# Feature map from two elementwise steps, and block-diagonal k^T v by one masked product, in a fused linear attention and expert kernel

## The chip, the cores and the metric

The kernel runs on one core of a Trainium2 chip, as one program and one launch. The metric is the device time in microseconds (us) from the first to the last instruction of that core; the time of a kernel is the median of its runs. A core has five engines with queues of their own: TensorE (PE in the profile) for matmuls, VectorE (DVE), ScalarE (ACT), GpSimd (POOL) and SyncE (SP), which here only starts transfers. Each engine works through its own list of instructions in a fixed order.

## The reference: what is computed

Linear attention over 8 batches x 8 heads x 576 tokens x 64 channels, and then a layer of 8 experts, in which every token goes through all experts and the results are weighted by a matrix P. P comes from a Sinkhorn normalisation: eight rounds of dividing rows and columns by their sums.

```python
def phi(x):
    return np.where(x > 0, x, np.exp(x) - 1.0) + 1.0
q_p, k_p = (phi(q), phi(k))
kv = np.einsum('bhsd,bhse->bhde', k_p, v)
z = np.sum(k_p, axis=2)
num = np.einsum('bhsd,bhde->bhse', q_p, kv)
den = np.einsum('bhsd,bhd->bhs', q_p, z)[..., None] + 1e-06
return (num / den).astype(np.float32)
...
logits = x @ w_gate          # x: the attention's output, 4608 tokens x 512
P = np.exp(logits - logits.max())
for _ in range(8):
    P /= P.sum(1, keepdims=True) + 1e-09
    P /= P.sum(0, keepdims=True) + 1e-09
    P *= N / E
for e in range(E):           # 8 experts
    h = np.maximum(x @ w1[e], 0.0)
    out += P[:, e:e + 1] * (h @ w2[e])
```

The feature map phi(x) is x + 1 where x is positive and exp(x) elsewhere. It can be written without a comparison, in two ways: max(x + 1, min(exp(x), 1)) and min(exp(x), max(x + 1, 1)). For x > 0 both give x + 1, since exp(x) is the larger; for x <= 0 both give exp(x).

## The kernel before

The kernel has two parts. In the **front** the attention runs in 16 groups of four heads (two groups for each batch), and expert 0 runs between them as plain matmuls, so that PE has work while the other engines prepare the next group. After the front, experts 1 to 7 run in a form with fewer multiplications (Strassen's: seven block products in place of eight, with sums of blocks built by DVE); these are the lines L640 and L843 of the profile. A small planner in the kernel places each piece of work on an engine and in an order, from a table of priorities (`ranks`) at its end; where a piece names two engines, the planner or the table chooses.

One group of the attention, with cuts. The load, the feature map of k and of q, and v:

```python
# p_in, p_t, p_vv ...: pools of two buffers each; e: three
(nc.gpsimd if n in (2, 3) else nc.sync).dma_start(out=gr["tile"]..., in_=AP(...))   # k, q, v of the group
...
def f_e(_, ge=ge, nm=nm):                       # ScalarE
    ge["tile"] = fp.tile([P, 2, NJ, D], FP16, tag="e", ...)
    nc.scalar.activation(out=ge["tile"], in_=gin[nm]["tile"], func=AF.Exp)          # L266

def f_t(e, g_=gt[nm], nm=nm):                   # chosen: nothing here, or x + 1 on ScalarE
    g_["tile"] = fp.tile([P, NJ, 2, D], FP16, tag="t" + nm, ...)
    g_["on"] = e
    if e == "act":
        nc.scalar.add(out=..., in_=gin[nm]["tile"], add=1.0)                         # L272

def f_m(_, ge=ge, g_=gt[nm], nm=nm):            # VectorE
    nc.vector.tensor_scalar(out=ge["tile"], in0=ge["tile"], scalar1=1.0, ..., op0=ALU.min)   # L275
    o = g_["tile"].rearrange("p j r d -> p r j d")
    if g_["on"] == "act":
        nc.vector.tensor_tensor(out=o, in0=o, in1=ge["tile"], op=ALU.max)            # L278
    else:
        for r in range(2):
            nc.vector.scalar_tensor_tensor(out=o[:, r], in0=gin[nm]["tile"][:, r], scalar=1.0,
                                           in1=ge["tile"][:, r], op0=ALU.add, op1=ALU.max)   # L281
...
def f_v(e):
    copy(e, gvv["tile"][:, :, :, 0:D], gin["v"]["tile"])    # v as fp16, with a column of ones for z
```

k^T v of two heads at a time, both as one 128 x 130 product, of which only the two blocks on the diagonal are wanted; they are copied into a tile whose other blocks were zeroed once:

```python
gkv, gz = [S_.grp(p_ye[2]), S_.grp(p_ye[3])], S_.grp(p_kvz)
def f_kv(_):
    for j in range(NJ):
        for hh in range(2):
            nc.tensor.matmul(gkv[hh]["tile"], lhsT=gt["k"]["tile"][s, j, :, :]..., rhs=gvv["tile"][s, :, j, :], ...)  # L309
for hh in range(2):
    for rr in range(2):
        def f_z(e, rr=rr, hh=hh):
            s = slice(64 * rr, 64 * rr + 64)
            copy(e, gz["tile"][s, hh, rr, :], gkv[hh]["tile"][s, rr, :])             # L221 or L223
```

Then q is transposed on PE (`qt_ps`, L335), the denominator (`den_ps`, L350) and the numerator (`num_ps`, L374) are multiplied out of q and the tile `kvz`, the quotient is formed on DVE (`xn`, L379), and transposed once more into `xT` (`xt_ps`, L390), from which the experts read. Expert 0 on a block of 512 tokens is `hq` = w1^T x (L546, 32 matmuls of 128x512), relu on ACT (L550), and `ye` = h w2 (L736, 32 matmuls), copied to an accumulator. The accumulator is scaled by P once P is known:

```python
def f_s(_, tt=tt, gg=gg):
    nc.vector.tensor_scalar(out=acc[g][:, tt, :], in0=acc[g][:, tt, :], scalar1=P_sb[:, gg, 0:1], ..., op0=ALU.mult)  # L757
...
tf = add(("dve", 0.49), f_s, deps=[tf, p_done], prio=NG + g - 400.0)
```

The weights w1 and w2 of expert 0 are loaded in two halves each through GpSimd's queue, in this order of that queue: w1, inputs of group 2, inputs of group 3, w2. At the very start PE runs matmuls on zeros (`yw`, L481), which only keep it busy.

Of the kernel before, what the change touches and what calls it, by code (L numbers as in the profile page):

```python
# [122 lines left out]
def kernel(  # L123
# [17 lines left out]
    P = 128  # L141
# [37 lines left out]
    kvz_t = [fp.tile([P, 2, 2, D + 1], FP16, tag=f"kvz{i}", name=f"kvz{i}", bufs=1) for i in range(2)]  # L179
# [57 lines left out]
    def att(b, g):  # L237
# [22 lines left out]
        for nm in "kq":  # L260
            ge = S_.grp(p_e)
            gt[nm] = S_.grp(p_t[nm])

            def f_e(_, ge=ge, nm=nm):
                ge["tile"] = fp.tile([P, 2, NJ, D], FP16, tag="e", name="e" + nm, bufs=3)
                nc.scalar.activation(out=ge["tile"], in_=gin[nm]["tile"], func=AF.Exp)  # L266

            def f_t(e, g_=gt[nm], nm=nm):
                g_["tile"] = fp.tile([P, NJ, 2, D], FP16, tag="t" + nm, name="t" + nm)
                g_["on"] = e  # L270
                if e == "act":
                    nc.scalar.add(out=g_["tile"].rearrange("p j r d -> p r j d"), in_=gin[nm]["tile"], add=1.0)  # L272

            def f_m(_, ge=ge, g_=gt[nm], nm=nm):
                nc.vector.tensor_scalar(out=ge["tile"], in0=ge["tile"], scalar1=1.0, scalar2=None, op0=ALU.min)  # L275
                o = g_["tile"].rearrange("p j r d -> p r j d")
                if g_["on"] == "act":
                    nc.vector.tensor_tensor(out=o, in0=o, in1=ge["tile"], op=ALU.max)  # L278
                else:
                    for r in range(2):  # L280
                        nc.vector.scalar_tensor_tensor(out=o[:, r], in0=gin[nm]["tile"][:, r], scalar=1.0,  # L281
                                                       in1=ge["tile"][:, r], op0=ALU.add, op1=ALU.max)
            te = fadd(("act", 1.17), f_e, deps=[tin[nm]], acq=[ge], use=[gin[nm]], prio=pr)
            tt_ = fadd({"dve": 0.6, "act": 1.17}, f_t, deps=[tin[nm]],
                       acq=[gt[nm]], use=[gin[nm]], prio=pr)
            tph[nm] = fadd(("dve", 1.35), f_m, deps=[te, tt_], use=[ge, gt[nm], gin[nm]], prio=pr)
# [8 lines left out]
        tvv.append(fadd(("act", 1.17) if n < 2 else ("dve", 0.75), f_v, deps=[ta, tin["v"]],  # L295
# [5 lines left out]
        gkv, gz = [S_.grp(p_ye[2]), S_.grp(p_ye[3])], S_.grp(p_kvz)  # L301

        def f_kv(_):
            for hh in range(2):
                gkv[hh]["tile"] = yps.tile([P, 2, D + 1], FP32, tag=f"ye{2 + hh}", name=f"kv_ps{hh}")
            for j in range(NJ):
                for hh in range(2):
                    s = slice(64 * hh, 64 * hh + 64)
                    nc.tensor.matmul(gkv[hh]["tile"], lhsT=gt["k"]["tile"][s, j, :, :].rearrange("p r d -> p (r d)"),  # L309
                                     rhs=gvv["tile"][s, :, j, :], start=(j == 0), stop=(j == NJ - 1))  # L310
        def f_za(_):
            gz["tile"] = kvz_t[(len(p_kvz["order"]) - 1) % 2]
        tza = fadd(("none", 0.0), f_za, deps=[tph["k"]] + tvv, acq=[gz], prio=pr)
        tkv = fadd(("pe", 0.6), f_kv, deps=[tph["k"], tza] + tvv, acq=gkv, use=[gvv, gt["k"]], prio=pr)

        tz = []
        for hh in range(2):
            for rr in range(2):
                def f_z(e, rr=rr, hh=hh):
                    s = slice(64 * rr, 64 * rr + 64)  # L320
                    copy(e, gz["tile"][s, hh, rr, :], gkv[hh]["tile"][s, rr, :])
                tz.append(fadd({"dve": 0.23, "act": 0.22}, f_z, deps=[tza, tkv], use=[gkv[hh], gz], prio=pr))
# [165 lines left out]
    for i in range(34):  # L488
        twa = add(("pe", 0.3), lambda e, n=2 if 4 <= i < 17 else 1: f_warm(e, n), deps=[twa], use=[gyw], prio=900.0, after=1.2 + 0.5 * i)
    for i in range(2):  # L490
        nc.vector.memset(vv_t[i][:, :, :, D], 1.0)
        nc.vector.memset(kvz_t[i], 0.0)
# [16 lines left out]
    def f_close(_):  # L509
# [4 lines left out]
        accp.append(ctx.enter_context(tc.tile_pool(name="combo", bufs=2)))  # L514
        for i, n in enumerate(("ye2", "ye3")):
            Zt[i] = yps.tile([P, 2, 256], FP32, tag=n, name=f"Z{n}")
# [191 lines left out]
    def unit_plain(e, g, gW=None, tW=None):  # L708
# [36 lines left out]
        for tt in range(1 if e > 0 else 0, 4):  # L745
# [10 lines left out]
            def f_s(_, tt=tt, gg=gg):  # L756
                nc.vector.tensor_scalar(out=acc[g][:, tt, :], in0=acc[g][:, tt, :],  # L757
                                        scalar1=P_sb[:, gg, 0:1], scalar2=None, op0=ALU.mult)
            if e == 0:
                tf = add({"act": 0.59, "dve": 0.69}, f_fin, deps=[ty[tt], t_close if g >= NA else None],  # L760
                         use=[gy[tt]], prio=g - 400.0)
                tf = add(("dve", 0.49), f_s, deps=[tf, p_done], prio=NG + g - 400.0)
# [166 lines left out]
    for tt in (3, 2, 1, 0):  # L929
# [5 lines left out]
        43:-88.9997 46:-94.9994:act 55:-94.9991:dve 56:-94.9985:dve 66:4.15 68:-94.9985 71:-89.0006  # L935
        74:-392.9979:dve 85:-89.0003:dve 92:3.7509:dve 96:-97.9985 99:-94.9991:dve 107:-392.9967
        110:-95.0006:act 133:-94.9991 139:-95 146:4.1497 152:-88.9994 153:-94.9994:dve 154:-94.9997
        166:-95.0003:act 172:-398.0018:dve 173:4.1497:dve 174:-97.9988:dve 199:-398.0021 200:-94.9988
        209:-88.9991 216:-94.9973 226:-94.9991 235:-94.9997 246:-90.9976:dve 248:-94.9997 255:-95.0003:act
        256:-90.9973:act 257:-397.9985:act 261:-94.9997 263:-95.0003 265:-397.9994 267:-392.9982 269:-398  # L940
        284:-95.0003:dve 286:-95 288:-398.0024 290:-95.0009 294:-392.9976:act 296:-95.0042:dve 298:-95.0003
        299:-98:dve 300:-94.9991 305:-95.0006 307:-95.0003 309:-397.9988 310:-392.9997 311:-393.0006 321:-95
        323:-95.0006 324:-88.9994 326:-95 328:-88.9997 331:-90.9982 334:-392.9985:act 338:-94.9991 340:-94.9997
        343:-97.9997 349:-89.9994 350:-95.0015:dve 353:8.3497 362:-97.9997:act 366:-88.9985 370:-95.0006
        376:-94.9994 377:-90.9985:dve 378:-88.9988 379:-90.0012:act 383:-95.0006 385:-90.9985 387:-88.9991
        392:-90.0018:dve 403:-94.9979:act 406:-95.0009 408:-88.9988 411:-85.0009:dve 414:-89.0009 416:-88.9991
        418:-88.9994 421:-90.0018 423:-395.0012 427:-95.0018 429:-90.0018 444:-88.9997 446:-88.9985
        447:-97.9991:act 448:-90.9997:act 454:-85.0009 459:-89.0012 461:-90.9988 463:-90.9982 467:-95.0018
        476:-90.0012:dve 482:-90.0015 486:-94.9973:act 487:-90.0009:act 488:-89:act 490:-89.9997
        491:-95.0015:act 492:-95.0009 493:-90.0012:dve 494:-395 499:-85.0015 501:-90.9985 505:-99.003  # L950
        516:-95.0012:act 526:-89.0003:act 532:-395.0015 533:-94.9988 534:-90.9985 535:-395.0021 540:-90.9979
        543:-394.9994 545:-395.0006 554:-90.0012 563:-395.0012 565:-395.0012:dve 569:-90.9982 571:-85.0015
        573:-89.9997 576:-96.0006 578:-96 580:-90.9979 585:8.3482:dve 593:-90.9976:act 595:-85.0006
        601:-395.0024 607:-89.0021 609:-90.9985 616:3.75 618:-95.0042 630:-89.0003 640:-88.9988 646:-96.0009
        647:-395.0015:dve 648:-395.0012 650:-395.0009 653:-395.0018 655:-97.9994 659:3.7515 666:8.3485
        671:-90.9985 678:8.7491 684:8.6479 717:-99.003 723:-95.0009 725:-94.9994:dve 731:-398.0021:act
        733:3.7509 735:-98 742:-94.9994 744:-94.9991 749:-95.0003 754:-94.9994 756:-94.9991 759:-398.0003
        762:-95.0003 763:-95.0003 764:-97.9997 768:-90.0012:act 769:8.3491 774:8.6485 776:8.6488 791:-94.9976
        793:-90.0009 796:-90.0015 797:-90.9985 799:-89.0006 800:4.1515 801:-88.9991 803:-95.0006 804:-95.0003
        806:-89.9988 809:-90.0012:act 816:3.7512 818:-395.0006 824:-90.9988 826:-90.0018 830:-395 836:-90.0012  # L960
        838:-395.0009 839:-90.9985 840:-89.0009 844:-395.0018 845:-89.0006 850:-94.9982:act 854:-94.9979:act
        856:-395.0006 865:-88.9994 866:-90.0009 867:-90.9979 868:-88.9997 875:-395.0024 897:8.3494 898:3.75
        906:-85.0009 910:8.6509 916:-89 918:3.7494 920:-85.0012 924:3.7509 926:-395.0033 928:3.7497 929:-90.9994
        931:8.6512 938:-96.0015 947:1.7518 957:-395.0015 959:-96.0027 961:-96.0006 964:8.3488 969:8.3494
        979:3.7518 988:-90.9988 990:-90 992:8.3491 998:-395.0021 1000:3.7512 1006:3.7479 1009:8.7488 1010:8.7482
        1016:3.7512:act 1017:8.6518 1020:8.7503 1031:8.7494 1039:-85.0012 1041:-94.9997 1043:-90.9994
        1049:3.7518 1051:-95.0012 1052:8.6491 1060:8.3479 1061:8.6482
    """
    for w in ranks.split():
# [3 lines left out]
        if en:  # L973
            t["eng"] = {en[0]: t["eng"][en[0]]}
# [31 lines left out]
```

The softmax here doesn't subtract the row's maximum and nothing guards it: scores larger than these inputs give would overflow.

## Time and profile before

| | before |
|---|---|
| median of 3 runs | 972.1 us |
| lowest and highest | 971.19 and 972.13 us |
| span of the profiled run | 970.4 us |
| granted TensorE clock, mean | 0.999 |
| first matmul of expert 0 (L546) | 21.21 us |
| first block product of the Strassen form's second layer (L843) | 202.08 us |
| scalings of the accumulator by P (L757) | 36, all on DVE, 488 ns each |

How to read it: "busy" is the time in which an engine has an instruction in work. Several matmuls can be in work at once, and their ends are modelled, so PE's busy time can be full while PE does not run at its best; the starts of its matmuls tell more. A group of instructions has one line in the program (L266, say), an engine, an operation, the tiles it writes and reads, their shapes, a count, the busy time and the mean of one. After the bar stands the idle time of that engine just before these instructions, and after an arrow what ended most of it. The chain of waits is followed back from the last instruction: at each step to what released it, or to the one before it on its engine.

### The profile page before, as it was taken

How to read it: one execution, taken by the hardware profiler on the slowest of the kernel's cores; microseconds unless marked ns; L12 is line 12 of the kernel's file. 1: busy time of each engine (PE TensorE's matmuls, PEld its weight loads, DVE VectorE, ACT ScalarE, POOL GpSimd, SP SyncE). 2: the span in 40 equal slices, each digit the busy share in tenths (PEclk: the TensorE clock that was granted, in tenths of full speed). 3: DMA queues.
4: the chain of work that ended last, by engine and by line, in shares of the span. 5: the costliest groups of instructions: out<-in, count | busy, mean ns of one | idle time of the engine just before them, and what ended most of it. 6: DMA issues, size and time to landing. Idle time of an engine off the chain costs nothing.

```text
span 970.4 us, 21442 instructions
## 1 busy us (share of the span) xinstructions
PE 959.5 (99%) x8737; PEld 794.4 (82%) x8737; DVE 776.5 (80%) x1563; ACT 575.0 (59%) x1049; POOL 112.2 (12%) x158
## 2 busy tenths in 40 slices
PE   8999999999999999999999999999999999999998
PEld 4556564588888888888888888888888888888886
DVE  6899868988887888878887888878887888877775
ACT  6799945465555555555555555555555555555553
POOL 3000000101111111111111111111111111111110
PEclk9999999999999999999999999999999999999999
DMA  9986925472226222272226222272226322235554
GB/s 312 265 271 243 243 73 207 155 162 76 78 76 138 99 74 74 79 152 78 73 75 138 98 73 78 76 161 77 78 77 137 104 77 77 77 96 166 163 163 110
DMA packets 47188, 121.99 MB, mean 126 GB/s; under 512 B 4208, under 2 KB 18288, under 8 KB 47088
## 3 DMA queue, kind: packets, MB, share of 16 engines
q1 hardware_dynamic: 32208, 99.76, 30.2%
q0 software_dynamic: 14480, 20.33, 11.8%
q8 instruction: 68, 1.11, 0.4%
q10 hardware_dynamic: 400, 0.52, 0.2%
q14 instruction: 32, 0.26, 0.1%
HBM read 119.69 MB, written 17.69 MB: 142 GB/s over the span
## 4 chain that ended last, share of the span: by engine, by line
PE 92%; DMA 3%; ACT 3%; DVE 1%; issue 1%; POOL 0%; ACTq 0%; DVEq 0%; POOLq 0%
PE ye L843 33%; PE hq L640 23%; PE att L640 11%; PE ye L736 6%; PE Zye L640 6%; PE Zye L843 6%; PE hq L546 4%; DMA w<-in_moe_w_dram 2%; PE yw L481 1%; DMA kin<-in_k_dram 1%; PE xt_ps L390 1%; ACT eq L266 1%; ACT h L550 1%; PE kv_ps L309 1%; PE num_ps L374 1%
## 5 line engine op out<-in xcount | busy, mean ns | idle before, releaser
L857 DVE SCALAR_TENSOR_TENSOR acc<-ye,P_sb,acc 128x256 f32<-128x256 f32 x620 | 267.2, 479 | 128.2 <-PE ye L843 127.7
L640 PEld LDWEIGHTS <-W 128*128 128x128 f16 x2016 | 197.2, 98 | 23.6
L843 PEld LDWEIGHTS <-S 128*128 128x128 f16 x1984 | 194.1, 98 | 22.5
L843 PE MATMUL ye<-T,S 128*128 128x256 f16 x1488 | 192.9, 273 | 0.0
L640 PEld LDWEIGHTS <-w 128*128 128x128 f16 x1512 | 147.9, 98 | 18.5 <-issue 0.8
L666 ACT ACTIVATE h<-hq 128x512 f16<-128x512 f32 x126 | 75.2, 597 | 144.1 <-PE hq L640 144.1
L843 PEld LDWEIGHTS <-h 128*128 128x128 f16 x1488 | 145.6, 98 | 16.9
L867 POOL TENSOR_TENSOR acc<-acc,st 128x256 f32<-128x256 f32 x124 | 87.5, 727 | 621.4 <-ACT st L864 562.5
L640 PE MATMUL hq<-xs,W 128*128 128x256 f16 x1008 | 151.3, 273 | 0.0
L640 PE MATMUL att<-xs,W 128*128 128x256 f16 x1008 | 151.3, 273 | 0.0
L640 PE MATMUL hq<-xs,w 128*128 128x256 f16 x1008 | 141.0, 273 | 0.4 <-DVE h L669 0.3
L663 ACT ACTIVATE h<-Zye 128x512 f16<-128x512 f32 x126 | 75.2, 597 | 40.6 <-PE Zye L640 40.6
L864 ACT ACTIVATE st<-Zye,P_sb 128x256 f32<-128x256 f32 x124 | 52.0, 470 | 78.3 <-PE Zye L843 78.3
L669 DVE CUSTOM_DVE_ANT_0 h<-att,s 128x512 f16<-128x512 f32 x126 | 86.6, 687 | 11.4 <-ACT s L656 11.0
L656 ACT COPY s<-hq 128x512 f32<-128x512 f32 x126 | 73.4, 583 | 36.7 <-PE hq L640 36.7
L816 DVE TENSOR_TENSOR S<-h 128x1024 f16<-128x1024 f16 x124 | 85.2, 687 | 12.3 <-ACT h L666 12.3
L669 DVE CUSTOM_DVE_ANT_0 h<-hq,s 128x512 f16<-128x512 f32 x126 | 86.6, 687 | 0.2
L652 ACT COPY Zye<-hq 128x512 f32<-128x512 f32 x126 | 73.2, 581 | 17.5 <-PE hq L640 17.5
L736 PE MATMUL ye<-w,h 128*128 128x512 f16 x312 | 75.6, 379 | 1.9 <-DMA w<-in_moe_w_dram 1.4
L640 PE MATMUL Zye<-xs,w 128*128 128x256 f16 x504 | 75.7, 273 | 0.0
L660 ACT COPY s<-att 128x512 f32<-128x512 f32 x126 | 74.7, 593 | 0.0
L546 PE MATMUL hq<-xT,w 128*128 128x512 f16 x288 | 70.3, 379 | 0.9 <-ACT h L550 0.7
(95 smaller groups left out, 961.2 us busy)
## 6 DMA issues: line engine op xcount, KB each, us to landing
xs<-xd SPq DMA_DIRECT2D x63, 896.0 KB, 4.6
w<-in_moe_w_dram POOLq DMA_DIRECT2D x14, 1024.0 KB, 11.4
out_dram<-acc SPq DMA_DIRECT2D x67, 128.0 KB, 2.4
kin<-in_k_dram SPq DMA_DIRECT2D x14, 576.0 KB, 5.8
qin<-in_q_dram SPq DMA_DIRECT2D x14, 576.0 KB, 5.5
vin<-in_v_dram SPq DMA_DIRECT2D x14, 576.0 KB, 5.8
xd<-xst SPq DMA_DIRECT2D x9, 512.0 KB, 2.7
xd<-xT SPq DMA_DIRECT2D x9, 256.0 KB, 3.1
```

The source lines that it names most:

```text
L546: nc.tensor.matmul(ghq["tile"], lhsT=gw1["tile"][:, c, ts(f, P)], rhs=xT[:, c, ds(512 * g, 512)], start=(c == 0), stop=(c == NDT - 1))
L640: nc.tensor.matmul(dst[:, p, :], lhsT=lhs(p, c), rhs=rhs(c), start=(first and p == 0 and c == 0), stop=(c == 1), skip_group_check=True)
L656: nc.scalar.copy(out=gs2["tile"], in_=gX["tile"])
L660: nc.scalar.copy(out=gs5["tile"], in_=gR["tile"])
L663: nc.scalar.activation(out=hd(0, 0), in_=Zt[1], func=AF.Relu)
L666: nc.scalar.activation(out=hd(1, 0), in_=gX["tile"], func=AF.Relu)
L669: nc.vector._custom_dve(TENSOR_ADD_SAT, out=dst, in0=ps, in1=sb, s0=3.0e38, s1=0.0)
L736: nc.tensor.matmul(gy[tt]["tile"], lhsT=gh["tile"][:, f, ds(P * tt, P)], rhs=gw2["tile"][:, f, :], start=(f == 0), stop=(f == NFT - 1))
L816: nc.vector.tensor_tensor(out=Sx[:, i], in0=a0, in1=a1, op=op)
L843: nc.tensor.matmul(bank(g_)[:, s, :], lhsT=lhs(s, kk), rhs=rhs(kk), start=(new and s == 0 and kk == 0), stop=(kk == 3), skip_group_check=True)
L857: nc.vector.scalar_tensor_tensor(out=dst(), in0=bank(g_)[:, s, :], scalar=P_sb[:, gg, e:e + 1], in1=dst(), op0=ALU.mult, op1=ALU.add)
L867: nc.gpsimd.tensor_tensor(out=dst(), in0=dst(), in1=gst["tile"], op=ALU.add)
```

## The change

Three things are changed in the front.

1. The feature map takes the second form, min(exp(x), max(x + 1, 1)). One DVE instruction with two scalars makes max(x + 1, 1) straight from the input, and a second one takes the minimum with the exponential. The separate minimum with 1 goes, and ScalarE no longer makes x + 1 for some tensors. The aim is less elementwise work and a first step that needs no exponential.
2. The four copies of diagonal blocks become one multiplication of the whole product by a mask `diag` (ones on the blocks, zeros elsewhere), made once. For that, k^T v gets a pool of its own with one tile over two PSUM banks, and the tiles `Z` of the later stage a pool that takes these banks over.
3. More pieces may run on either ScalarE or VectorE (the cast of v, the scaling by P), and the table of priorities is new, so that the order and the engine of many pieces in the front differ.

```diff
-    kvz_t = [fp.tile([P, 2, 2, D + 1], FP16, tag=f"kvz{i}", name=f"kvz{i}", bufs=1) for i in range(2)]
+    kvps = front.enter_context(tc.tile_pool(name="kvps", bufs=1, space=PSUM))
+    diag = fp.tile([P, 2, D + 1], FP16, tag="diag", name="diag", bufs=1)
+    p_kv = S_.pool(1)
...
-            def f_t(e, g_=gt[nm], nm=nm):
+            def f_t(_, g_=gt[nm], nm=nm):
                 g_["tile"] = fp.tile([P, NJ, 2, D], FP16, tag="t" + nm, name="t" + nm)
-                g_["on"] = e
-                if e == "act":
-                    nc.scalar.add(out=g_["tile"].rearrange("p j r d -> p r j d"), in_=gin[nm]["tile"], add=1.0)
-
-            def f_m(_, ge=ge, g_=gt[nm], nm=nm):
-                nc.vector.tensor_scalar(out=ge["tile"], in0=ge["tile"], scalar1=1.0, scalar2=None, op0=ALU.min)
+                nc.vector.tensor_scalar(out=g_["tile"].rearrange("p j r d -> p r j d"), in0=gin[nm]["tile"],
+                                        scalar1=1.0, scalar2=1.0, op0=ALU.add, op1=ALU.max)
+
+            def f_m(_, ge=ge, g_=gt[nm]):
                 o = g_["tile"].rearrange("p j r d -> p r j d")
-                if g_["on"] == "act":
-                    nc.vector.tensor_tensor(out=o, in0=o, in1=ge["tile"], op=ALU.max)
-                else:
-                    for r in range(2):
-                        nc.vector.scalar_tensor_tensor(...)
+                nc.vector.tensor_tensor(out=o, in0=o, in1=ge["tile"], op=ALU.min)
...
-        tvv.append(fadd(("act", 1.17) if n < 2 else ("dve", 0.75), f_v, ...))
+        tvv.append(fadd({"act": 1.15, "dve": 0.76}, f_v, ...))
...
-        gkv, gz = [S_.grp(p_ye[2]), S_.grp(p_ye[3])], S_.grp(p_kvz)
+        gkv, gz = S_.grp(p_kv), S_.grp(p_kvz)
...
-                    copy(e, gz["tile"][s, hh, rr, :], gkv[hh]["tile"][s, rr, :])     # four times
+            nc.vector.tensor_tensor(out=gz["tile"],
+                                    in0=gkv["tile"][:, :, 0:2 * (D + 1)].rearrange("p h (r d) -> p h r d", r=2),
+                                    in1=diag[:, None, :, :].broadcast_to([P, 2, 2, D + 1]), op=ALU.mult)
...
-                tf = add(("dve", 0.49), f_s, deps=[tf, p_done], prio=NG + g - 400.0)
+                tf = add({"act": 0.6, "dve": 0.49}, f_s, deps=[tf, p_done], prio=NG + g - 400.0)
...
-    ranks = """ ... (the table before)
+    ranks = """ ... (a longer table)
```

The numbers beside the engine names ("dve", 0.49) are the planner's own estimates, by which it orders the work.

## The prediction

> **What bounds the kernel now.** I first read the busy table of the page, then the same counts by stretch of time.
>
> ```profile
> PE 959.5 (99%) x8737; PEld 794.4 (82%) x8737; DVE 776.5 (80%) x1563; ACT 575.0 (59%) x1049; POOL 112.2 (12%) x158
> ```
>
> TensorE (PE) is the bound on average. The table by stretches (columns: stretch, its sum, busy us and instructions of each engine, granted clock, DMA share, GB/s) shows that this does not hold equally everywhere.
>
> ```profile
> 60.00:70.00 10.00, 9.68 (x107) 5.86 (x101) 9.66 (x23) 9.80 (x18) 0.00 (x0) 1.00 0.76 262
> 70.00:80.00 10.00, 9.94 (x99) 5.96 (x98) 9.49 (x20) 9.89 (x18) 0.00 (x0) 1.00 0.87 315
> 150.00:160.00 10.00, 10.00 (x51) 4.87 (x50) 8.39 (x26) 5.57 (x10) 0.00 (x0) 1.00 0.64 212
> 300.00:600.00 300.00, 300.00 (x2750) 268.87 (x2749) 242.35 (x466) 169.58 (x319) 40.24 (x56) 1.00 0.35 99
> ```
>
> From 300 to 600 us PE runs 2750 matmuls in 300 us, 0.109 us each, without a hole. The change does not touch that part. In the front, at 60 to 80 us, VectorE (DVE) and ScalarE (ACT) are both 95 to 99% busy: there the three engines are level. The busy column overstates PE, because the modelled ends of its matmuls fill short holes. So I took the starts from the timeline of PE and subtracted from each start-to-start distance the usual one of its kind (0.216 us for 128x512, 0.055 for transposes and the numerator, 0.031 for k^T v, 0.026 for the denominator). What is left is idle PE: about 5.4 us in the first 20 us, 4.0 us from 20 to 38.7, 5.3 us from 38.7 to 130, and nothing that can be told from 130 to 200. Everything that this change can win is in these 15 us.
>
> The timeline of PE and the chain of waits show one hole that no vector work can fill.
>
> ```profile
> 35.91 0.44 PE L390 MATMUL xt_ps<-ident,xn 128*128 128x128 f16 x5
> 37.79 1.02 PE L736 MATMUL ye<-w,h 128*128 128x512 f16 x4 [1.45 <-DMA w<-in_moe_w_dram]
> ...
> 12.96 1.07 ACT eq L266
> 14.05 0.47 DVE eq L275
> 14.80 1.72 issue
> 16.53 0.70 POOL qin L253
> 17.24 0.71 POOL vin L253
> 17.94 0.74 POOL w L207
> 18.68 19.07 DMA w<-in_moe_w_dram
> ```
>
> PE waits 1.45 us for the second half of expert 0's w2. It was issued at 18.68 us and landed 19.07 us later, because the DMA engines work without a pause from 2 to 41 us. **This landing at 37.75 us is a gate**: the front before it is limited by DMA, the front after it by three level engines.
>
> **What the Trainium skill says.** "VectorE: DVE Perf Modes", in its perf-mode tier table, gives tensor_scalar four elements per cycle for 16-bit data and two for fp32 in SBUF, tensor_tensor two for 16-bit and one from PSUM in fp32. The trace agrees: on the same 1152 elements the f16 minimum takes 450 ns, the f32 cast 746, the f16 tensor_tensor 758, and the three-operand instruction needs 754 for only 576. "DMA: Bandwidth & Descriptors", section on queues, rings and completion order, says that each DMA engine goes round robin between the queues that have work. The trace fits it: w2 (GpSimd's queue) took its 19 us while SyncE's queue moved other tensors. "Perfetto Trace Analysis" warns in its opening note that matmul busy time is a bad metric because matmuls are pipelined; hence the start-to-start count.
>
> **The change part by part.** Durations are of these rows (groups of the first 125 us):
>
> ```profile
> L281 DVE SCALAR_TENSOR_TENSOR tk<-kin,ek 128x576 f16<-128x576 f32 x18 | 12.8, 755 | 0.3
> L223 DVE CAST vv<-vin 128x1152 f16<-128x1152 f32 x14 | 10.4, 746 | 0.0
> L275 DVE TENSOR_SCALAR ek<-ek 128x1152 f16<-128x1152 f16 x16 | 7.2, 450 | 4.5 <-ACT ek L266 4.5
> L278 DVE TENSOR_TENSOR tq<-tq,eq 128x1152 f16<-128x1152 f16 x7 | 5.3, 758 | 1.1 <-ACT tq L272 0.7
> L223 DVE CAST kvz<-kv_ps 64x65 f16<-64x65 f32 x22 | 4.5, 215 | 2.0 <-PE kv_ps L309 1.6
> L272 ACT ACTIVATE tk<-kin 128x1152 f16<-128x1152 f32 x7 | 8.2, 1169 | 0.1
> L221 ACT CAST kvz<-kv_ps 64x65 f16<-64x65 f32 x38 | 7.6, 208 | 3.4 <-DVE kvz L223 1.6 <-PE kv_ps L309 1.2
> ```
>
> *Feature map*, 32 tensors (16 groups, k and q). Before, 18 of them (the 36 calls of the first row and its twin for q, two for one tensor) cost DVE 0.450 + 2 x 0.754 = 1.96 us; 14 cost DVE 0.450 + 0.758 = 1.21 and ACT 1.165. After, every one costs DVE 0.746 (the cast row stands in: same shape and types, one source) + 0.758 = 1.50 and ACT nothing. DVE: 18 x 1.96 + 14 x 1.21 = 52.2 becomes 32 x 1.50 = 48.1, so -4.1 us. ACT: -14 x 1.165 = -16.3 us. The first of the two instructions no longer waits for the exponential, so a k tensor is ready about 0.450 + 1.51 - 0.758 = 1.2 us sooner after it.
>
> *k^T v*: 64 corner copies (24 on DVE, 40 on ACT in the whole program) become 16 multiplications of 128x260 out of PSUM. For these I take the 128x256 normalisation out of PSUM, 0.42 us. DVE: 16 x 0.42 - 24 x 0.215 = +1.5; ACT: -40 x 0.208 = -8.3. The denominator matmuls wait for one instruction instead of four on two engines.
>
> *Choices moved by the new order*, counted in the instruction order of both programs: v casts on DVE 14 to 7 (DVE -5.2, ACT +8.0 at 1.148); copies of expert 0's output to DVE 1 to 8 (DVE +4.8, ACT -4.1); transposed copies shift by four (DVE about 0, ACT about 0).
>
> *Sum over the front*: DVE -4.1 + 1.5 - 5.2 + 4.8 = **-3 us**, ACT -16.3 - 8.3 + 8.0 - 4.1 = **-21 us**. ACT gets a fifth of its front time back; DVE stays almost as full as it is. None of this is on the path by itself: PE's instructions are the same 8737, so the time can only fall by PE idle.
>
> *After 130 us*: 21 of the 36 scalings of the accumulator (488 ns each) go from DVE to ACT, but PE has no idle there, so nothing is won. The extra PSUM pool only renames the same eight banks.
>
> **On the path.** Up to the gate, PE's order after the change holds the same work before the first matmul that needs w2's second half: 32 layer-one matmuls, 8 of layer two, four groups of k^T v. So what PE has still to do when the gate opens is the same, and a gain of 1 to 3 us before it only makes PE wait longer. Does the gate move? The issue of w2 waits behind k, q and v of group 3, which wait for buffers; faster reading frees them up to 2 us sooner, but w2 stands in a queue that is full anyway. The same sooner release lets SyncE issue group 4's k before 24.75 us, by 1.5 to 2 us in my estimate, and those bytes share the engines with w2. From 24.75 us to the landing at 37.75 GpSimd's queue moved what alone takes 8 us (two input tensors, which land 1.5 us apart at the start of the trace, and two halves of w2, 2.5 us each as w1's did): 8 of 13 us, 0.6 of the engines. So that head start costs w2 some 0.4 x 1.75 = 0.7 us. I expect the gate at **38.5 us, +0.7**.
>
> After the gate, 5.3 us of idle. Of it 1.4 us is fixed: 12 holes of 0.118 us behind the last k^T v matmul of each group, which come whatever follows. Another 2.9 us lies in 11 holes over 0.1 us (waits for ACT's relu and for copies; the longest are 0.52, 0.41 and 0.41), and 1.0 us in small ones. An ACT that is a fifth freer and a shorter way to the denominator should remove about two thirds of those 3.9: **-2.5 us**. Other terms: the order draws attention further into expert 0 (group 16's k^T v after 320 instead of 296 expert matmuls) and ends the routing's column sums closer to the first eviction that needs them; a small wait there, **+0.1 us** on average. Sum: -2.5 + 0.7 + 0.1 = -1.7, so 972.1 - 1.7 = **970.4 us**.
>
> **Rivals.** (a) *The gate takes all*: w2 lands 2 us later and the idle after it stays, as DVE stays 90 to 95% busy and becomes the lone bound of the front. For it: DVE loses only 3 of the 100 us that it is busy in the first 125. Time 972 to 974. (b) *The order is worth more than the load*: all 3.9 us go, and the gate stays or comes a little sooner: -3.9 to -5, time 967 to 968. For it: each of these holes is a latency that the new order shortens. (c) *The routing becomes the wait*: DVE carries the first scalings after the probabilities, and evictions of the first Strassen unit come late; +1 to +3 us, time 971 to 974. Against it: some 7 us of matmuls still stand between the last column sum and the second product of that unit.
>
> **Range and chances.** (b) sets the low end and (a) the high end; a few tenths are the spread of the runs (971.19 to 972.13). Eight in ten: 967.5 to 973.0. A change of 2% is 19.4 us, more than all 15 us of PE idle in the front, so faster by over 2% is all but excluded (0.01), and slower by as much would take a stall that nothing here suggests (0.01).
>
> **What would show it.** Right: ACT's busy time falls by about 21 us before 130 us, DVE's by about 3; the two-scalar row near 746 ns and the k^T v row near 420; PE still waits for w2, at 38 to 39 us and for longer than 1.45; idle PE after it near 3 us; the part from 210 us on as long as before. Wrong: w2 landing 2 us sooner (a larger gain), a two-scalar row of 1.2 us (DVE as the bound, no gain), or a wait of PE for the probabilities or for accumulator evictions around 195 to 210 us.

## The result and the profile after

| | before | after |
|---|---|---|
| median | 971.64 us (971.09 to 972.13) | **979.83 us** (979.03 to 980.15) |
| after / before | | **1.0074**, 95% interval 1.0057 to 1.0091 |
| span of the profiled run | 970.4 us | 978.4 us |
| granted TensorE clock, mean | 0.999 | 0.994 |

The change makes the kernel 0.74% slower (the two medians by themselves give 0.84%, inside the interval), above the predicted range, which ended at 973.0 us. The spans differ by 8.0 us, and that is the sum to be explained.

First the busy row of TensorE (PE) and its granted clock in 40 slices of the span, from the page of after.

```profile
PE 960.5 (98%) x8737; PEld 794.7 (81%) x8737; DVE 765.9 (78%) x1517; ACT 567.9 (58%) x1016; POOL 111.0 (11%) x158
...
PEclk9799999999999999999999999999999999999999
```

PE has the same 8737 instructions. VectorE (DVE) and ScalarE (ACT) are both less busy than before (776.5 and 575.0 us), and the kernel is slower nevertheless. The clock has one dent, in the second slice (24 to 49 us). The table by stretches (stretch, its sum, busy us and instructions of PE, PEld, DVE, ACT, POOL, granted clock, DMA share, GB/s) shows what lies there.

```profile
20.00:30.00 10.00, 9.18 (x78) 4.73 (x77) 8.64 (x16) 9.76 (x15) 1.01 (x1) 1.00 1.07 350
30.00:40.00 10.00, 1.21 (x24) 0.90 (x24) 0.62 (x2) 1.08 (x2) 0.00 (x0) 0.77 1.15 306
40.00:50.00 10.00, 10.00 (x71) 5.65 (x70) 5.80 (x12) 3.58 (x5) 0.00 (x0) 0.72 0.16 33
```

From 31 to 40 us all engines stand almost still and only DMA works. From 40 to 50 PE looks full, but runs 71 instructions at a clock of 0.72. The timeline of PE (start, us, instruction, count, in brackets the wait before it and what ended it) names the wait.

```profile
30.29 0.69 PE L303 MATMUL kv_ps<-vv,tk 64*128 64x130 f16 x18
39.77 1.86 PE L729 MATMUL ye<-w,h 128*128 128x512 f16 x4 [8.79 <-DMA w<-in_moe_w_dram]
...
42.07 1.91 PE L729 MATMUL ye<-w,h 128*128 128x512 f16 x4
```

The chain of waits (start, us, what) tells how long that transfer was under way.

```profile
9.43 8.06 DMA w<-in_moe_w_dram
17.49 0.28 issue
17.77 21.96 DMA w<-in_moe_w_dram
39.73 0.04 issue
39.77 1.86 PE ye L729 x4
```

PE waits 8.79 us for w2 in front of its *first* layer-two matmul (L729); before, it waited 1.45 us in front of its ninth. The four matmuls at 39.77 and at 42.07 take 1.86 and 1.91 us, where four usually take 1.02: they start 0.427 us apart instead of 0.216.

The rows that answer to those shown of before (line, engine, operation, tiles, shapes, count | busy us, mean ns | idle before, and what ended it):

```profile
L272 DVE TENSOR_SCALAR tk<-kin 128x1152 f16<-128x1152 f32 x16 | 11.9, 746 | 3.7 <-DMA kin<-in_k_dram 3.5
L277 DVE TENSOR_TENSOR tk<-tk,ek 128x1152 f16<-128x1152 f16 x16 | 11.9, 748 | 1.0 <-ACT ek L268 0.8
L310 DVE TENSOR_TENSOR kvz<-kv_ps,diag 128x260 f16<-128x260 f32 x16 | 6.8, 423 | 2.1 <-PE kv_ps L303 1.9
L753 DVE TENSOR_SCALAR acc<-acc,P_sb 128x512 f32<-128x512 f32 x15 | 6.5, 480 | 0.0
```

And the scalings that went to ACT:

```profile
L751 ACT ACTIVATE acc<-acc,P_sb 128x512 f32<-128x512 f32 x21 | 14.4, 738 | 0.0
```

The arithmetic costs what the prediction said: 746 ns for the two-scalar instruction, 748 for the minimum, 423 for the masked product.

Last, the idle time of PE, counted as in the prediction (start-to-start distances less the usual one of each kind, so matmuls at a low clock count as idle too):

| stretch | before | after | difference |
|---|---|---|---|
| 0 to 38.7 us | 9.35 | 13.95 | +4.60 |
| 38.7 to 60 us | 1.91 | 3.35 | +1.44 |
| 60 to 130 us | 3.43 | 1.92 | -1.51 |
| 130 to 200 us | -0.66 | -0.31 | +0.35 |
| 200 to 250 us | 0.16 | 3.39 | +3.23 |
| sum | 14.19 | 22.30 | **+8.1** |

(A small negative sum means that the usual distance is taken a little too large there.) The 8 us come from two places: the landing of w2 with the low clock behind it, about 6 us before 60 us, and 3.2 us behind 200 us, where the Strassen form begins. Between them the change gains 1.5 us.

### The profile page after: what moved, and what is told of

It reads as the page before. It is cut to its first block, busy times and chain, and to the rows that moved or that the text cites. A ratio compares the mean times of both kernels' runs of the same rounds, so it can differ in the third digit from the quotient of the medians.

```text
span 978.4 us, 21349 instructions
## 1 busy us (share of the span) xinstructions
PE 960.5 (98%) x8737; PEld 794.7 (81%) x8737; DVE 765.9 (78%) x1517; ACT 567.9 (58%) x1016; POOL 111.0 (11%) x158
## 4 chain that ended last, share of the span: by engine, by line
PE 91%; DMA 4%; ACT 3%; issue 0%; DVE 0%; SPq 0%; ACTq 0%; POOLq 0%
PE ye L839 32%; PE hq L633 22%; PE att L633 11%; PE ye L729 7%; PE Zye L633 5%; PE hq L539 5%; PE Zye L839 5%; DMA w<-in_moe_w_dram 3%; ACT acc L751 1%; PE xt_ps L381 1%; PE num_ps L365 1%; DMA vin<-in_v_dram 1%; PE kv_ps L303 1%; PE qt_ps L326 1%; ACT eq L268 0%
## 5 line engine op out<-in xcount | busy, mean ns | idle before, releaser
L729 PE MATMUL ye<-w,h 128*128 128x512 f16 x312 | 77.9, 387 | 8.8 <-DMA w<-in_moe_w_dram 8.8
L645 ACT COPY Zye<-hq 128x512 f32<-128x512 f32 x126 | 73.3, 582 | 16.0 <-PE hq L633 16.0
```

The lines of the kernel that those rows point to most:

```text
L729: nc.tensor.matmul(gy[tt]["tile"], lhsT=gh["tile"][:, f, ds(P * tt, P)], rhs=gw2["tile"][:, f, :], start=(f == 0), stop=(f == NFT - 1))
```

## The experiments

The first theories were these. **Theory 1**: the new table of priorities exchanged the two halves of w2 on GpSimd's queue, so that the half PE needs first lands last. **Theory 2**: the routing's pieces come late, and P with them; this makes the holes behind 200 us. **Theory 3**: it is the scalings by P, as a block of work, that make them. **Theory 4**: the inputs that SyncE issues sooner hold up w2. The runs below are compared with before on their own chip, where its median was 973.0 to 974.3 us; so ratios count, and "span" is that of the profiled run. Before itself ran there at a granted clock of 0.998 or less in 12 of 30 to 19 of 39 executions (medians 975.1 to 975.9 us, the others 972.0 to 972.7) and e4_queue and e13_queue_swapped never did, so part of their gain in the ratio is that; against before's other executions they gain 2.4 and 1.4 us. (Some recorded expectations number otherwise: "theory 3" in that of e8_mapkv is that the new order is what costs, and "theory 2 in its second form" in that of e9_dvescale is theory 3 here.)

| run | ratio to before, 95% interval | span, us |
|---|---|---|
| after | 1.0074 (1.0057 to 1.0091) | 978.4 |
| e1_halves | 1.0019 (1.0008 to 1.0030) | 974.8 |
| e2_sink | 1.0279 (1.0240 to 1.0318) | 1001.2 |
| e3_both | 1.0257 (1.0225 to 1.0290) | 996.5 |
| e8_mapkv | 1.0011 (0.9997 to 1.0026) | 973.0 |
| e4_queue | 0.9959 (0.9944 to 0.9974) | 967.5 |
| e9_dvescale | 0.9964 (0.9944 to 0.9983) | 968.6 |
| e11_mapkv_queue | **0.9949** (0.9934 to 0.9965) | 967.4 |
| e10_bq | 0.9972 (0.9959 to 0.9985) | 968.8 |
| e5_fill | 1.0059 (1.0043 to 1.0076) | 976.3 |
| e13_queue_swapped | 0.9971 (0.9961 to 0.9980) | 968.7 |
| e12_lowscale | 0.9959 (0.9942 to 0.9976) | 967.8 |
| e14_map_queue | 0.9957 (0.9940 to 0.9975) | 967.9 |
| e17_no_scalings | 0.9933 (0.9913 to 0.9953) | 965.4 |
| e15_early_p | 1.0034 (1.0022 to 1.0046) | 976.4 |

### e1_halves: w2's halves in the old order

```diff
     # load of a weight in two parts; cut == 1 is w2
+    i = 1 - i if cut == 1 else i
```

The two loads keep their places in the queue; only what they carry is exchanged.

> The changed kernel with one edit: the two halves of expert 0's w2 are loaded in their old order (first half first); every queue's order stays. Theory 1 (the swapped halves make the 9.0 us hole): the first layer-two matmul waits only for the earlier landing, near 34.1 us, and does 2.7 us of work before the later landing at 39.7; PE's clock no longer falls, so the 12 matmuls at 0.427 us go back to 0.216 (2.5 us). Together -5.2: 974.6 us. Rival (the front is bound by VectorE and ScalarE anyway, so that a smaller hole comes back as other waits): 978 to 980 us.

Measured: 3.6 us less than after, in the span and in the median (976.2 us; before was slower on this chip, so the ratios differ by more, 0.55%). The timeline of PE:

```profile
34.21 1.02 PE L730 MATMUL ye<-w,h 128*128 128x512 f16 x4 [2.39 <-DMA w<-in_moe_w_dram]
...
39.81 1.84 PE L730 MATMUL ye<-w,h 128*128 128x512 f16 x4 [2.80 <-DMA w<-in_moe_w_dram]
```

PE now starts layer two at the first landing (34.17 us) and waits again for the second (39.77). One hole of 9 us has become two, of 5.2 us together; the matmuls in between are work that the exchange had kept waiting. The gain is 3.6 us and not the 5.2 expected, because the clock fell again: the four matmuls behind the second wait take 1.84 us. Theory 1 holds, but the landings themselves have not moved: 39.77 us here, 39.73 in after, 37.75 in before.

### e2_sink and e3_both: P earlier

```diff
     for w in ranks.split():
         n, p, *en = w.split(":")
+        if 602 <= int(n) <= 626:     # the Sinkhorn pieces keep their old priority
+            continue
```

e3_both has the edit of e1_halves too.

> The changed kernel with one edit: the 25 pieces of the Sinkhorn rounds get back their old high priority, so that P is ready near 185 us instead of 204; the swapped halves stay, 18 scalings stay on ScalarE. Theory 2 (P comes so late that the scalings on ScalarE and VectorE meet the first products of the Strassen form): the holes between 205 and 230 us, 3.2 us together, go: 976.6 us. Rival (it is the scaling on ScalarE itself, whenever it comes): holes stay, 979 to 980 us.

> Both edits of the two runs before. If the two causes are independent the gains add: 979.8 - 5.2 - 3.2 = 971.4 us. If one hides the other (PE catches up later what it lost), less than the sum: 974 to 975 us.

Measured: 23 us more than after instead of less. The edit did make P early (written at 190.27 us, where after has 203.66), but it did not test the theory, because two new stalls appeared. Two of PE's waits in e2_sink (us in total, times, longest):

```profile
PE att L633 <- ACT s L653: 13.3, 1, 13.3
...
PE ye L729 <- ACT h L543: 6.3, 1, 6.3
```

And one of ACT's:

```profile
ACT s L649 <- DMA xd<-xT: 12.8, 1, 12.8
```

As soon as P is known the scalings become free, and their priority stands above everything: 13 of them (8.07 us) run on ACT ahead of a relu (L543) that PE needs, and 18 on DVE ahead of the differences L572, whose stores out of xT must be done before that memory is used again. So the run says nothing on theory 2, but something on theory 3: where the scalings land in one block ahead of work that PE needs, PE pays. e3_both shows the same two stalls (11.7 and 6.3 us) with the gain of e1_halves (2.9 us of waiting for w2 in place of 7.2).

### e8_mapkv: the new arithmetic in the old order

Before's table of priorities, engines and queues, with the new feature map, and one masked multiplication in the place of the last of the four copies.

> The kernel before with its own order, and only the two new pieces of arithmetic put into it: the feature map in two instructions, k^T v masked by one multiplication (at the place of the last of the four copies). Theory 3 (the arithmetic is good, the new order is what costs): 969.5 to 971.5 us, w2 still landing near 37.8 us. Rival (the arithmetic itself loads VectorE, since it moves x + 1 from ScalarE): 973 to 976 us.

Measured: the same time as before, or a little more. That is in the range of the rival, but not for its reason, a loaded VectorE: the same arithmetic gains when w2 lands early (e11_mapkv_queue, below). SyncE's queue shows what happens (start, us, transfer). In before it issues the k and q of group 4 here:

```profile
24.75 0.37 SPq L253 DMA_DIRECT2D kin<-in_k_dram  x1
26.58 0.37 SPq L253 DMA_DIRECT2D qin<-in_q_dram  x1
```

In after, which has the same arithmetic as e8_mapkv:

```profile
21.30 0.37 SPq L255 DMA_DIRECT2D kin<-in_k_dram  x1
23.33 0.37 SPq L255 DMA_DIRECT2D qin<-in_q_dram  x1
```

The faster map reads its inputs sooner, the buffers come free sooner, and the inputs of group 4 are issued 3.5 us sooner, beside w2; e8_mapkv issues the first of them at 21.05 us. In it w2's halves land at 34.77 and 40.45 us, where before has 31.90 and 37.75. PE has holes of 2.35 and 0.61 us there and about 1.7 us of low clock. So the change's arithmetic by itself, without its table, moves the gate by 2.7 us, and what it gains elsewhere is used up.

### e4_queue and e13_queue_swapped: the inputs of groups 4 and 5 behind w2

```diff
-                (nc.gpsimd if n in (2, 3) else nc.sync).dma_start(
+                (nc.gpsimd if n in (2, 3, 4, 5) else nc.sync).dma_start(
```

e4_queue has this and the edit of e1_halves; e13_queue_swapped has this alone.

> The run e1_halves with one edit more: the inputs of groups 4 and 5 are issued from GpSimd's queue, behind w2, in place of SyncE's queue. Theory 4 (a faster feature map frees the input buffers sooner, SyncE issues group 4 some 3 us sooner, and those bytes hold up w2): w2's second half lands near 32.5 us in place of 39.8, the 6.6 us of idle and slow clock at the first layer-two matmuls go; against the kernel before on the same chip from +1.9 us to about -4.7 us. Rival (GpSimd's own queue sets w2's pace, or PE then waits for group 4's inputs): the landing stays at 38 to 40 us or a new wait for group 4 comes, +1 to +3 us.

> The kernel after with the inputs of groups 4 and 5 issued behind w2 on GpSimd's queue, as in e4_queue, but with w2's halves left in their exchanged order. By theory 1 the first half is now the last of that queue, as the second was in e4_queue, and lands near 32.6 us; PE comes to its first layer-two matmul at about 30.8 us, so a hole of 1.5 to 2 us is left instead of 9[...]: 1.5 to 2 us more than e4_queue, whose ratio was 0.9959, hence about 0.998. If the exchange costs more than the wait for its landing, the ratio is 1.000 or higher; if the landing is not set by the traffic of SyncE's queue, the hole stays at 7 us or more and the ratio is near 1.006.

Measured: both beat before. No input that SyncE issued is now on its way beside w2, whose halves land at 29.93 and 32.55 us in e4_queue, and at 29.61 and 32.15 in e13_queue_swapped. In the latter PE reaches its first layer-two matmul with the halves still exchanged, and does not wait at all:

```profile
31.50 0.69 PE L303 MATMUL kv_ps<-vv,tk 64*128 64x130 f16 x18
32.19 1.02 PE L729 MATMUL ye<-w,h 128*128 128x512 f16 x4
```

Between them e1_halves and these two runs fill a table of two by two, in spans: exchanged halves with SyncE's inputs 978.4 (after), old halves 974.8, exchanged halves with the inputs behind w2 968.7, both mended 967.5. The exchange costs 3.6 us while w2 is late. When w2 is early, 1.2 us are left between the last two. In these traces they lie in the first 20 us (idle 4.48 against 3.29; w1's first half landed 0.9 us later in e13_queue_swapped), so that PE came to w2 only at 32.19 us, just after the landing at 32.15. In e4_queue it came at 31.00 us; with the exchange and that landing it would have waited some 1.1 us. So what the exchange costs when w2 is early is not told apart from luck at the start. **The root is the traffic beside w2**; the exchange made it worse. Theory 4 holds.

### e5_fill: PE busy while it waits

Forty matmuls of zeros in front of the first layer-two matmul, into the bank that this one overwrites.

```diff
     # layer two of expert 0, before its first matmul
+        for _ in range(40 if (e, g, tt) == (0, 0, 0) else 0):
+            nc.tensor.matmul(gy[tt]["tile"], lhsT=warm[:, 0:P], rhs=warm, start=True, stop=True)
```

> The kernel after with 40 matmuls of zeros (128x512) put in front of PE's very first layer-two matmul, into the bank that this matmul overwrites: they need nothing but the bank and fill the 9 us of waiting for w2 with 40 x 0.216 = 8.6 us of work. Nothing else is changed, w2 lands as late as before. If the low clock after the long hole has a cost of its own (12 matmuls at 0.427 us rather than 0.216, 2.5 us), it goes: 2.5 us less than after, a ratio to before of about 1.0045, and no matmul near 0.427 us after 40 us. If the slow matmuls come from something else that happens then, such as the weights' arrival or the traffic, they stay, and the ratio is that of after, 1.0074, or somewhat more.

Measured: 2.1 us less than after in the span; in the ratio 0.15%, which the interval alone would not separate. The table by stretches settles it:

```profile
30.00:40.00 10.00, 9.71 (x68) 4.80 (x66) 1.44 (x3) 1.87 (x3) 0.00 (x0) 1.00 1.14 312
40.00:50.00 10.00, 10.00 (x91) 5.79 (x91) 7.71 (x15) 5.64 (x8) 0.00 (x0) 1.00 0.30 92
```

The clock stays at 1.00, PE does 91 instructions from 40 to 50 us instead of 71, and no matmul starts 0.427 us after its neighbour. The DMA share in 30 to 40 us is the same, so the low clock came from the standing still, not from the traffic. The forty matmuls took 0.6 us longer than the wait (the first layer-two matmul starts at 40.37 us), which the gain of 2.1 already contains.

### e9_dvescale, e12_lowscale, e17_no_scalings, e15_early_p: the holes behind 200 us

All four start from e4_queue, which has 3.5 us of idle PE from 195 to 250 us. The timeline of ACT in after shows why one looks at the scalings first (L751; "x4" is four in a row):

```profile
212.48 2.56 ACT L751 ACTIVATE acc<-acc,P_sb 128x512 f32<-128x512 f32 x4
214.94 0.59 ACT L659 ACTIVATE h<-hq 128x512 f16<-128x512 f32 x1
215.41 0.60 ACT L645 COPY Zye<-hq 128x512 f32<-128x512 f32 x1
```

The copy L645, for which PE waits 0.60 us at 216, stands behind four scalings and a relu. PE's other waits there are 0.8 us for ACT's copies Zye (L874) and 0.8 us for sums S of DVE. The edits:

```diff
-  tf = add({"act": 0.6, "dve": 0.49}, f_s, deps=[tf, p_done], prio=NG + g - 400.0)
+  tf = add(("dve", 0.49), f_s, ..., prio=10.0 + g)                    # e9_dvescale
+  tf = add({"act": 0.73, "dve": 0.49}, f_s, ..., prio=10.0 + g)       # e12_lowscale, e15_early_p
+  (f_s emits nothing: accumulators stay unscaled)                     # e17_no_scalings
+  ranks of the Sinkhorn pieces and of the differences L572 left out   # e15_early_p, besides
```

e17_no_scalings leaves out the 36 multiplications by P of expert 0's output, so its time is that of a kernel with less work.

> The run e4_queue with the scalings by P on VectorE alone and at low priority, so that they spread over the first units of the Strassen form. Theory 2 in its second form (the 21 scalings on ScalarE, 0.73 us each, stand ahead of the copies that PE waits for): the 2.6 to 3.3 us of holes between 205 and 230 us shrink to under 1, so about 2.5 us less than e4_queue. Rival (P is simply too late, whichever engine scales): the holes stay or turn into waits for VectorE, same as e4_queue or 1 to 2 us more.

> e4_queue with the scalings by P allowed on both engines, as in the change, but ranked behind the Strassen form's own pieces (priority 10 + g in place of g - 400). The scalings then wait until the accumulators are next read. By theory 3 (the scalings in a block, all at once when P has become known late, are what delays copies and differences) the holes of 3.3 us between 198 and 242 us go, wholly or to under 1 us: 3 us less than e4_queue, a ratio of 0.993. The rival, that e9_dvescale bore out for DVE alone: the work has to be done before the accumulators are used, wherever it is ranked, so holes of 0.7 us come back at each unit, and the ratio stays near 0.996.

> e4_queue without the 36 scalings of the accumulators by P (15 on DVE, 21 on ACT): the orders of all other instructions stay, and expert 0's output is added unscaled. If the scalings, which stand in a block ahead of the copies and differences that PE waits for, are what makes the holes of 3.3 us between 197 and 216 us, the idle of PE from 195 to 250 us falls to under 0.3 us, and the ratio from e4_queue's 0.9959 to 0.9925. If the late end of the column sums itself (their DVE instructions, or the accumulators that are first read late) makes the holes, two or more of those 3.3 us stay, and the ratio is 0.995 or higher.

> e4_queue with the new priorities of the Sinkhorn pieces and of the differences (L572) left out, so that P is ready some ten us sooner with the differences' stores done soon after it, and the scalings on both engines behind the other pieces (priority 10 + g). The expert's last plain matmuls then still run while the scalings are done. If late P is what makes the scalings collide with the Strassen form's first copies, the holes go, idle from 195 to 250 us falls under 0.5 us, and the ratio to about 0.9925, the best of all. If the order of the differences was what the new priorities were for, the stall of e2_sink returns (ACT waiting for the stores of xd, more than 5 us) and the ratio is over 1.0; if any place of 36 scalings costs PE some of its copies, 1 to 3 us stay and the ratio is 0.994 to 0.996.

Measured: PE's longest wait behind 195 us (190 in the last) in each, from its waits. In e9_dvescale:

```profile
PE ye L840 <- DVE S L813: 2.1, 3, 0.7
```

In e12_lowscale:

```profile
PE ye L840 <- DVE S L813: 1.9, 1, 1.9
```

In e17_no_scalings:

```profile
PE ye L842 <- DVE S L815: 0.7, 1, 0.7
```

In e15_early_p:

```profile
PE att L634 <- ACT s L654: 4.8, 1, 4.8
```

With the scalings on DVE the waits for ACT's copies go, and DVE's sums S come late in their place: idle 3.4 us. With low priority on both engines the idle is 2.9 us, most of it in one hole of 2.1. Without the scalings 0.9 us is left, and the span is 2.1 us shorter. So the scalings make about 2.5 of the 3.5 us, and in this order, with P late, neither DVE alone nor a low priority cures it. Theory 3 holds for these 2.5 us, except that being a block is not shown to be what hurts; the sums S on DVE, late without any scaling, make the rest.

The remaining question is why before has room. There P is written 21.6 us before the first product of the Strassen form's second layer (L843, at 202.88 us in the timeline; the 202.08 in the table of before is not that matmul's start):

```profile
181.30 0.46 DVE L463 TENSOR_TENSOR P_sb<-wt,Rr 128x288 f32<-128x288 f32 x1
181.79 10.38 DVE L757 TENSOR_SCALAR acc<-acc,P_sb 128x512 f32<-128x512 f32 x26
```

In after it is 4.0 us:

```profile
203.66 0.46 DVE L454 TENSOR_TENSOR P_sb<-wt,Rr 128x288 f32<-128x288 f32 x1
...
207.64 1.04 PE L839 MATMUL ye<-w,h 128*128 128x256 f16 x8
```

Before runs 26 scalings in one block of 10.38 us on DVE without a hole of PE behind 195 us, and e11_mapkv_queue, in the same order, has the 36 scalings on DVE and 0.2 us of idle. e15_early_p was to give that room back, with P at 183.62 us; but ACT then runs nine scalings and one copy without a pause from 189.4 to 195.5 us in front of the copies of s, waits 0.7 us more for the stores from xT, and PE waits 4.8 us and then runs at a clock of 0.73 from 200 to 210 us. **So that late P leaves the scalings no room is what the traces suggest; no run shows that an earlier P alone would cure it in the new order.** In this order early P twice made things worse (e2_sink with e3_both, and e15_early_p), each time with 16 or 18 of the scalings on ACT. Early P with all scalings on DVE, as before has it, was not run in the new order.

### e10_bq, e14_map_queue, e11_mapkv_queue: what the arithmetic is worth

Before's own order, with the inputs of groups 4 and 5 behind w2: alone (e10_bq), with the new map (e14_map_queue), and with map and masked product (e11_mapkv_queue).

> The kernel before with nothing but the inputs of groups 4 and 5 on GpSimd's queue behind w2. Theory 4: its one hole of 1.45 us goes, w2 lands near 32.5 us: -1.5 us, no more, because PE comes to that place at 36.3 us only. So the move of the queue is worth less without the new arithmetic than with it. Rival (the move is worth as much by itself): -4 us or more.

> The kernel before with the new feature map alone (old order, old copies of the diagonal blocks), and the inputs of groups 4 and 5 on GpSimd's queue. The queue alone (e10_bq) gave 0.9972, the queue with map and masked multiplication (e11_mapkv_queue) 0.9949. If the map carries the gain, this run stands near 0.9955 and the idle of PE from 40 to 130 us falls as there; if the one multiplication in place of four copies carries it (a shorter way to the denominator), it stands near 0.997.

> The run e8_mapkv (both new pieces of arithmetic in the order of the kernel before) with the inputs of groups 4 and 5 on GpSimd's queue behind w2. Theory 4: the holes at w2 (2.3 and 0.6 us, and 1.7 us of slow clock behind them) go: from +1.1 us against the kernel before to about -3.5 us. Rival as for e4_queue: no change.

Measured: the queue alone brings 0.28%, with the map 0.43%, with both 0.51%, the lowest ratio of the runs that do the whole work, though not clear of the next. The steps between them (0.15% and 0.08%) lie within the intervals, and the spans say 0.9 and 0.5 us. PE's idle from 38.7 to 130 us gives the larger step to the masked product (6.26 us, about 6.0 with the map, 5.37 with both), so which of the two carries the gain is not settled. Clear is one thing: the k of group 4 is issued at 24.57 us in e10_bq and at 21.26 in e14_map_queue, so it is the map that frees the input buffers 3.3 us sooner, and behind w2 this does no harm: w2's last half lands at 32.68, 32.62 and 32.59 us.

What is left in e11_mapkv_queue, from PE's waits:

```profile
PE ye L738 <- ACT acc L223: 1.4, 1, 1.4
...
PE den_ps L350 <- DVE kvz L319: 0.8, 1, 0.8
```

A version with e4_queue's front (2.8 us of idle from 38.7 to 130 us, against 5.4 here) and this tail would have neither loss; it was not built.

## Why the prediction was wrong

**The bound and the gate: right.** PE idle in the front decides, and w2's landing is the gate. About 6 of the 8 us went there.

**"Up to the gate, PE's order after the change holds the same work before the first matmul that needs w2's second half": this step failed.** It was read from PE's order alone. Which half of w2 GpSimd's queue loads first was not read, and the new table had exchanged them. So the eight layer-two matmuls and what follows from them, counted as work ahead of the gate, stood behind it. e1_halves shows this step's size: 3.6 us, of which about 1.0 is a shorter stretch of low clock (idle from 38.7 to 60 us 2.3 instead of 3.35).

**"I expect the gate at 38.5 us, +0.7": right mechanism, mis-sized.** It is 39.73 us, +2.0; e8_mapkv, with the arithmetic alone, has +2.7. The term that was too small is what the sharing costs. GpSimd's queue was taken to need 0.6 of the engines, an average from 24.75 us on, so that it would lose 0.4 of the head start. But from the landing of group 3's v the two halves of w2 take 2.41 and 2.62 us in e4_queue, where SyncE's inputs are not beside them, and 5.53 and 5.63 in after: they get less than half. Before's own trace already has 4.12 and 5.85 us. The 2.0 us are thus 0.8 of a later v (28.57 against 27.78 us) and 1.4 of the first half, less 0.2. The head start, put at 1.5 to 2 us, is 3.45 in after, but 2.4 in e1_halves and e5_fill, whose gate lies at 39.77 and 39.71 all the same; its size does not set the gate alone. Two queues that share the engines are what the Trainium skill lets one expect ("DMA: Bandwidth & Descriptors", section on queues, rings and completion order: an engine goes round robin between queues that have work). The page gives no share; the prediction cited it and then reckoned with 0.6.

**What a late gate costs: a term was missing.** The prediction counted only the wait. After 8.98 us without a matmul PE ran some 5.7 us with matmuls 0.427 us apart; idle from 38.7 to 60 us is 3.35 us in after and 1.00 in e13_queue_swapped, so the low clock cost 2.4 us. "TensorE: Matmul & The Clock Gate" (Part 1) states 426.7 ns cold against 215.7 warm at 512 columns; the trace agrees, with 427 and 216.

**"After the gate ... -2.5 us": right in size, not in its reason.** From 38.7 to 130 us the idle was to fall from 5.3 to about 2.8 us. In after itself it is 5.28, of which the low clock is 2.4; in e4_queue and e13_queue_swapped, where the clock stays full, it is 2.78 and 2.76. The prediction gave the credit to ACT's free time and the shorter way to the denominator. With the same queues and the old order, that arithmetic takes the idle from 6.26 us (e10_bq) to 5.37 (e11_mapkv_queue), 0.9 us; the other 2.6 came with the new table, its order and its choice of engines. So the size was met partly by luck.

**Rival (c), "+0.1" for the routing: wrong.** It is +3.2 us. It named the wait (evictions of the first Strassen unit) and the place, and set it aside because "some 7 us of matmuls still stand between the last column sum" and the second product. They do, from 200.95 us to 207.64. But P is written only at 203.66, and the scalings, which need P, start from 204.16 to 225.22 us, among the first products. The step that failed is that they cost nothing: "21 of the 36 scalings of the accumulator (488 ns each) go from DVE to ACT, but PE has no idle there, so nothing is won" asked what is won and not what is lost. They are 14.4 us of new work on an engine whose copies PE waits for. The move to ACT is not the whole cause, for with all of them on DVE (e9_dvescale) the idle is as large; e17_no_scalings puts about 2.5 us on the scalings of both engines. Why they cost nothing in before's order is not shown.

**The arithmetic: right.** Predicted 746, 758 and 420 ns, measured 746, 748 and 423. ACT's busy time in the whole program falls by 7.1 us; less the 14.4 us of new scalings, the rest falls by 21.5, where -21 was predicted. DVE falls by 10.6, of which the moved scalings are 8.8 (15.3 less 6.5), so the rest falls by 1.8, where -3 was predicted.

**The sum**: +0.7 became about +6 (gate, exchange and clock), -2.5 held, but showed in after only as -1.5 beyond 60 us, and +0.1 became +3.2. Rival (a) had the direction, for the gate took all; it had not the size.

## What to carry to other kernels

When an elementwise step gets faster, ask what its freed buffers will issue, and whether a transfer that gates the next stage is on the way then: here a map that frees its inputs 3.3 us sooner delayed the weights by 2 to 2.7 us, and putting those inputs behind the weights on the same queue turned a loss of 0.7% into a gain of 0.3%. When an order is changed, read every queue's order, the loads' too, and not only that of the engine that is the bound: which half arrives first is decided there. And work moved to an engine with much idle time still delays what stands behind it there: here a copy that PE needed stood behind four scalings of 2.56 us.

## What was not expected of the hardware

- TensorE's clock fell after holes much shorter than 9 us. In e1_halves the matmuls behind a wait of 2.80 us start 0.427 us apart, and in e8_mapkv those behind one of 2.18; in before, behind 1.45 us, and in e1_halves behind 2.39, they keep 0.216. "TensorE: Matmul & The Clock Gate" (Part 1) speaks of an idle window of about 3.4 us, so shorter holes would not be expected to do this. The traces show what decides. Their records of the clock have, between its first rise and the last fall, only durations that are whole multiples of 3.413 us (in after 9, 3 and 273 of them). Cut each of the 16 traces from that first rise on into stretches of 3.413 us, up to 955 us, and count PE's idle in each as above: at the end of the 10 full-clock stretches with 2.25 us or more of idle the clock was halved, and after the other 4404, with 2.17 us or less, it was not. So it is the idle within such a stretch that counts, with a limit between these two in these traces. The wait of 2.18 us in e8_mapkv lies with other holes in a stretch with 2.25 us of idle (30.55 to 33.96 us); that of 2.39 in e1_halves is cut by the end of a stretch at 33.04 us, and the stretch before that end has 2.17 us of idle, the one after it less. (2.17 and 2.25 are close enough for the count itself to blur them.)
- The same scaling of 128x512 f32 by one value for each partition takes 480 ns on DVE and 738 on ACT, so it is no even trade.
